# First tokens' gated product made early in C12's bank, and the completing product moved to second place

## The chip, the cores and the metric

The kernel runs on one core of one Trainium2 chip. The metric is the device time of one execution in microseconds; three runs of the kernel before took 3023.33, 3024.01 and 3027.07 us, median 3024.01. TensorE multiplies (PE in the profile; PEld is its weight loader), VectorE (DVE), ScalarE (ACT) and GpSimd (POOL) work on elements, SyncE (SP) issues DMAs. Each engine takes its instructions in order and waits at the first one that is not ready.

## The reference

Eight sequences of 3072 tokens by 256 features pass a Fourier mixing layer and then a gated feed-forward layer:

```python
X = np.fft.rfft(x, axis=1)
Yr = Xr @ w_r - Xi @ w_i + b_r ;  Yi = Xr @ w_i + Xi @ w_r + b_i
Yr, Yi = softshrink(Yr, 0.01), softshrink(Yi, 0.01)
y = np.fft.irfft(Yr + 1j * Yi, n=3072, axis=1)          # (8, 3072, 256)
out = ((y @ w_a) * (y @ w_b)) @ w_out                   # d_ff = 1536
```

## The kernel before

The Fourier part of a batch runs in small tasks: `f1` (16 of three 512-column matmuls), `f2` (12), `f3` (12 times two halves), `i1` (12) and `i2` (16). The feed-forward part takes most of TensorE's time. It works on pairs of token blocks of 2 x 384 tokens (32 pairs, four a batch) and, for each pair, on 12 blocks of 128 of the 1536 features: 384 steps, the function `step`. A step makes both gates a and b of its block for both halves of the tokens, a 2 x 2 block product, with seven products in place of eight (Strassen's scheme in Winograd's form).

A product, `run(k)`, is three matmuls of 384 columns (`mm3`: every operand is split in a high and a low half). The seven accumulate in three PSUM banks: X (two alternate, `x_ps`), `ya` and `yb`. Between them ScalarE copies a bank as it then stands to SBUF (`take`: s1, s2, s5) and VectorE adds. In the program before the order is

- run(0) into X, copy s1; run(1) into ya, c11 = s1 + ya (VectorE, in s1); a slot; `last_prod` of the step before;
- run(2) into X, copy s2; run(3) into yb, copy s5; output piece 0 of the step before; a slot;
- run(4) into X, then c22 = s5 + X (VectorE); run(5) into yb; output pieces 1 to 3 of the step before;
- then for the first 384 tokens: Y = yb + s2 in the bank, s1 = Y * s1 in SBUF (the gated product), and its split: ScalarE writes the high half h1, VectorE the low half l1 = s1 - h1.

`last_prod` adds the seventh product to X one step later, and makes the gated product and the split (h2, l2) of the last 384 tokens. Both halves of the tokens stand side by side in one tile g, a high one and a low one, of which there is one buffer (pool `p1`). `proj` multiplies g by a block of `w_out`, in four output pieces of three matmuls (the table `pieces`: bank, place in it, half of the 256 output features, first token, tokens); the third matmul of a piece is the one that reads the low half of g. The pieces collect over the 12 steps of a pair in three more banks.

A slot runs the next Fourier task. There are two in a step. Of the 372 steps after the first pair, 262 have a task in the second slot and 110 have none (75 of them have none in the first either); in 63 steps the first holds f2 and the second i1, and these follow steps that hold the two halves of f3.

The order on TensorE is that of the code. The order on the other engines is set by `Order`: a chain of operations is handed over where its input is issued; its urgent operations are issued when a model of the engines' times says that they can start, and the others when the model finds an engine free, or when `put` or `need` asks for them. `vacate` and `reads` say which operation of a chain is the last reader of a bank.

The result tile's pieces are copied out by `store` at the end of a pair. In the first pair (before 265 us) VectorE also decodes the feed-forward weights.

Of the kernel before, what the change touches and what calls it, by code (L numbers as in the profile page):

```python
# [12 lines left out]
F32 = mybir.dt.float32  # L13
# [9 lines left out]
P = 128  # L23
NJ = DFF // P
W = 384
# [230 lines left out]
def fft_mix_glu_kernel(ctx: ExitStack, tc: tile.TileContext, x, w_r, w_i, b_r, b_i, w_a, w_b, w_out, c1, m2, v, t2, out):  # L256
# [416 lines left out]
    def yr_sums(p):  # L673
        for k in ((0, 0), (0, 1), (1, 0)):
            od.put(yr[k][1])
        a11, a12, a21, a22 = (yr[k][0] for k in ((0, 0), (0, 1), (1, 0), (1, 1)))
        s3 = p6.tile([P, W], F32, tag="yr", name="yr")
        s2 = p6.tile([P, W], F32, tag="yr", name="yr")
        yr["c"] = od.chain(
            ("V", W, lambda e: tt(e, s3, a11, a21, ALU.subtract)),  # L680
            ("V", W, lambda e: tt(e, a21, a21, a22, ALU.add)),
            ("V", W, lambda e: tt(e, s2, a21, a11, ALU.subtract)),
            ("S", 0, lambda e: [yr_split(p, k) for k in range(RING - 7 if p else 0)]),
            spare=True,
        )
        yr["s"] = [a11, a12, s2, a21, s3, a12, a22]
        yr["pair"] = p
# [9 lines left out]
    def yr_split(p, k, urgent=0):  # L697
        if p == 0 and k < 2:
            s, c = yr[0, k]
            od.put(c)  # L700
        else:
            od.put(yr["c"], 1)
            s = yr["s"][k]
        h = state["ring"].tile([P, W], F32R, tag="ych", name="ych")
        l = state["ring"].tile([P, W], F32R, tag="ycl", name="ycl")
        ops = split(W, s, h, l)
        if k == 5:
            od.put(yc[p, 1][2])
            ops.insert(0, ("V", W, lambda e: tt(e, s, s, yr["s"][2], ALU.subtract)))
        yc[p, k] = h, l, od.chain(*ops, urgent=urgent, spare=True)  # L710
# [10 lines left out]

    weight_of = (0, 1, 5, 4, 6, 3, 2)
    gs = {}
# [11 lines left out]

    pieces = ((1, 2 * P, 1, 0, 2 * P), (0, 0, 0, 0, 4 * P), (2, 0, 1, 2 * P, 4 * P), (1, 0, 0, 4 * P, 2 * P))

    def proj(p, j, i):
# [11 lines left out]
        if j == 0:  # L750
# [6 lines left out]
            l[:, tok : tok + n],  # L757
            j == 0 and i < 3,
            j == NJ - 1,
# [6 lines left out]
    def store(p):  # L766
        osb = [p2.tile([P, 2 * W], F32, tag="osb", name="osb") for _ in range(2)]

        def take(d, tok, k, at, n):
            return ("AV", n, lambda e: copy(e, osb[d][:, tok : tok + n], o_ps[k][:, at : at + n]))  # L770

        def put(d):
            to = out[d * P : (d + 1) * P, 2 * W * p : 2 * W * (p + 1)]
            return ("S", 0, lambda e: nc.sync.dma_start(to, osb[d]))

        mid = 2 * P
        c = od.chain(
            take(0, 2 * mid, 1, 0, mid),
            take(1, 0, 1, mid, mid),
            take(0, 0, 0, 0, 2 * mid),  # L780
            put(0),
            take(1, mid, 2, 0, 2 * mid),
            put(1),
        )
        for k, left in enumerate((3, 4, 1)):
# [20 lines left out]
    def step(n, nxt):  # L806
# [26 lines left out]
        run(0, X, True)  # L833
        s1, c1_ = take(X)
        od.vacate(ya)
        run(1, ya, True)
        c11 = od.chain(add(s1, ya), urgent=1)
        od.reads(ya, c11, 0)
        slot()
        if n:  # L840
            last_prod(pp, pj)
        od.need(c1_)
# [6 lines left out]
        slot()  # L849
        od.need(c2_)  # L850
        run(4, X)
        od.put(c5_)
        held[p, j] = X, s5, od.chain(add(s5, X), urgent=1)
        od.need(c5_)
        run(5, yb)
        for i in range(1, 4):
            proj(pp, pj, i)
        if n:
            od.put(gs.pop((pp, pj))[3])
        h, l = (p1.tile([P, 2 * W], F32R, tag="g" + x, name="g") for x in "hl")  # L860
# [3 lines left out]
            ("V", W, lambda e: tt(e, Y, Y, s2, ALU.add)),  # L864
            ("V", W, lambda e: tt(e, s1, Y, s1, ALU.mult)),
            *split(W, s1, h1, l1, "VG"),
            urgent=2,
        )
        od.reads(yb, c, 2)
        gs[p, j] = [h, l, c, None]  # L870

    def f1_tasks(b):
# [190 lines left out]
```

## Time and profile before

| | |
|---|---|
| median of three runs | 3024.01 us |
| the profiled execution, its time | 3023.87 us |
| its span, first to last instruction | 3022.0 us |
| mean granted TensorE clock | 0.985 of full speed |
| busy: TensorE, VectorE, ScalarE, GpSimd | 2893.2, 2049.5, 1454.2, 874.1 us |

The rows below are from that one execution. A step takes some 6 to 8 us, by the tasks in its slots. Matmuls are pipelined: the listed duration of a matmul is longer than the distance to the next one, so lost time is read from distances between starts, or from the gaps of the weight loader (PEld).

### The profile page before, as it was taken

Reading aid. Unit: us, or ns where it says so; the run is one execution under the profiler, and the core shown is the slowest. Engines: PE = TensorE matmul, PEld = TensorE weight load, DVE = VectorE, ACT = ScalarE, POOL = GpSimd, SP = SyncE. Lnnn points to the kernel's source line nnn. Section 1 sums busy time; section 2 is a strip of 40 time slices with the busy share of each in tenths; the row PEclk is TensorE's granted clock in tenths of the full one; section 3 lists DMA queues with packets and bytes.
Section 4 is the critical chain, followed back from the end, with each engine's and each line's share of the span. In section 5 each row is a group of like instructions: output and inputs, shape, how many; then the busy total and the mean of one; then the engine's idle time right before and its main releaser. Section 6 shows DMA issues by size and latency. Waiting matters only on the chain.

```text
span 3022.0 us, 45662 instructions
## 1 busy us (share of the span) xinstructions
PE 2893.2 (96%) x16936; PEld 2667.2 (88%) x16936; DVE 2049.5 (68%) x3740; ACT 1454.2 (48%) x3226; POOL 874.1 (29%) x789
## 2 busy tenths in 40 slices
PE   5689999999999999999999999999999999999999
PEld 3568999899989999899998999989999899999998
DVE  7897676576765677666676676756676576766665
ACT  5454444544445444454445444454444544444443
POOL 4453331333322333223332223232232332310000
PEclk7889999999999999999999999999999999999999
DMA  6342111311113111221113211132112311110000
GB/s 184 117 123 69 55 36 54 94 59 57 41 51 109 39 61 36 78 83 39 55 39 100 73 41 46 56 95 62 52 36 62 94 57 52 41 40 26 26 11 22
DMA packets 123616, 186.55 MB, mean 62 GB/s; under 512 B 12320, under 2 KB 80768, under 8 KB 123392
## 3 DMA queue, kind: packets, MB, share of 16 engines
q1 hardware_dynamic: 120976, 177.26, 19.2%
q10 hardware_dynamic: 2416, 6.37, 0.7%
q8 instruction: 133, 2.18, 0.3%
q14 instruction: 91, 0.75, 0.1%
HBM read 108.08 MB, written 75.50 MB: 61 GB/s over the span
## 4 chain that ended last, share of the span: by engine, by line
PE 60%; issue 15%; DVE 12%; POOL 7%; ACT 5%; DMA 2%; DVEq 0%; ACTq 0%; POOLq 0%; SPq 0%
PE bank L290 60%; DVE g L284 3%; POOL zy L284 3%; POOL sx L284 2%; DVE s L284 2%; DVE zy L284 1%; ACT g L370 1%; DVE yr L284 1%; DVE bank L284 1%; POOL xs L284 1%; ACT s L824 1%; ACT sx L540 1%; POOL ycl L284 1%; ACT sx L534 0%; DMA m_in<-const_m_dram 0%
## 5 line engine op out<-in xcount | busy, mean ns | idle before, releaser
L824 ACT COPY s<-bank 128x384 f32<-128x384 f32 x1152 | 552.0, 484 | 1161.1 <-PE bank L290 1157.0
L284 DVE TENSOR_TENSOR s<-bank,s 128x384 f32<-128x384 f32 x1152 | 629.2, 556 | 535.3 <-PE bank L290 441.9
L284 DVE TENSOR_TENSOR bank<-bank,s 128x384 f32<-128x384 f32 x768 | 430.7, 561 | 49.9 <-PE bank L290 34.4
L284 POOL TENSOR_TENSOR ycl<-yr,ych 128x384 fp32r<-128x384 f32 x184 | 204.9, 1128 | 708.7 <-ACT ych L370 557.9
L284 DVE TENSOR_TENSOR g<-bank,g 128x384 fp32r<-128x384 f32 x384 | 213.1, 555 | 214.4 <-ACT g L799 214.4
L284 DVE TENSOR_TENSOR g<-s,g 128x384 fp32r<-128x384 f32 x384 | 268.7, 700 | 73.3 <-ACT g L370 71.2
L284 POOL TENSOR_TENSOR zy<-zy,zc 128x512 f32<-128x512 f32 x84 | 108.1, 1287 | 644.5 <-DVE zc L615 644.5
L284 POOL TENSOR_TENSOR x<-xin,x 96x512 fp32r<-96x512 f32 x104 | 137.6, 1323 | 414.7 <-PE bank L290 229.9
L290 PE MATMUL bank<-ych,wc2l 128*128 128x384 f32 x672 | 237.1, 353 | 2.2 <-DVE s L284 2.2
L290 PE MATMUL bank<-ych,wc0l 128*128 128x384 f32 x672 | 232.8, 346 | 3.2 <-ACT s L824 2.0
L290 PE MATMUL bank<-ych,wc3l 128*128 128x384 f32 x672 | 232.7, 346 | 0.8 <-DVE s L284 0.6
L290 PE MATMUL bank<-ych,wc1l 128*128 128x384 f32 x672 | 229.8, 342 | 0.0
L290 PE MATMUL bank<-ycl,wc0h 128*128 128x384 f32 x672 | 227.0, 338 | 0.0
L290 PE MATMUL bank<-ych,wc0h 128*128 128x384 f32 x672 | 226.8, 337 | 0.0
L290 PE MATMUL bank<-ycl,wc2h 128*128 128x384 f32 x672 | 226.5, 337 | 0.0
L290 PE MATMUL bank<-ycl,wc3h 128*128 128x384 f32 x672 | 226.3, 337 | 0.0
L290 PE MATMUL bank<-ycl,wc1h 128*128 128x384 f32 x672 | 226.3, 337 | 0.0
L290 PE MATMUL bank<-ych,wc2h 128*128 128x384 f32 x672 | 226.1, 337 | 0.0
L290 PE MATMUL bank<-ych,wc3h 128*128 128x384 f32 x672 | 226.0, 336 | 0.0
L290 PE MATMUL bank<-ych,wc1h 128*128 128x384 f32 x672 | 226.0, 336 | 0.0
L290 PE MATMUL bank<-wm_h,sx 128*128 128x256 f32 x1152 | 221.9, 288 | 4.0 <-DVE sx L284 4.0
L370 ACT CAST g<-s 128x384 fp32r<-128x384 f32 x384 | 197.6, 514 | 42.5 <-DVE s L284 39.9
(187 smaller groups left out, 6893.8 us busy)
## 6 DMA issues: line engine op xcount, KB each, us to landing
xin<-in_x_dram SPq DMA_DIRECT2D x128, 192.0 KB, 2.8
g_d<-gst SPq DMA_DIRECT2D x128, 192.0 KB, 2.1
gt<-g_d SPq DMA_DIRECT2D x96, 256.0 KB, 2.8
d_d<-dst SPq DMA_DIRECT2D x96, 256.0 KB, 2.1
dt<-d_d SPq DMA_DIRECT2D x64, 384.0 KB, 4.1
out_dram<-osb SPq DMA_DIRECT2D x64, 384.0 KB, 2.4
m_in<-const_m_dram SPq DMA_DIRECT2D x96, 128.0 KB, 2.1
t_in<-const_t_dram SPq DMA_DIRECT2D x64, 144.0 KB, 2.4
```

The lines of the kernel that those rows point to most:

```text
L284: (nc.vector if e == "V" else nc.gpsimd).tensor_tensor(o, a, b, op=op)
L290: nc.tensor.matmul(o, lhsT=l, rhs=r, start=start, stop=stop, **kw)
L370: ("a", n, lambda e: nc.scalar.copy(hi, w)),
L540: ("A", 512, lambda e: nc.scalar.copy(xh2, xsf)),
L824: return s, od.chain(("A", W, lambda e: nc.scalar.copy(s, q[:, :W])), urgent=1)
```

## The change

Seven things move. (1) run(4) and run(5) change places in the meaning of their operands: the one that completes C12 in yb now comes first, with its own weights and input (the list `yr["s"]` and `weight_of`; the difference a12 - s2 is now made for input 4). (2) The gated product of the first 384 tokens starts right behind it: Y + s2 and the product with s1 both stay in the bank yb, ScalarE casts h1 from the bank, and VectorE subtracts l1 from the bank. GpSimd is no choice for l1 any more. (3) The bank yb is now free for the next run(3) when l1 is done; before, when the product was in SBUF. (4) Output pieces are regrouped: pieces 0 and 1 take tokens 0 to 255 (256 columns each, one bank), pieces 2 and 3 tokens 256 to 767 (512 columns each). (5) Piece 1 moves ahead of run(4), pieces 2 and 3 stay last. (6) `last_prod` comes second in a step, right after run(0). (7) `store` copies by the new pieces.

```diff
--- before.py
+++ after.py
@@ -683,7 +683,7 @@
             ("S", 0, lambda e: [yr_split(p, k) for k in range(RING - 7 if p else 0)]),
             spare=True,
         )
-        yr["s"] = [a11, a12, s2, a21, s3, a12, a22]
+        yr["s"] = [a11, a12, s2, a21, a12, s3, a22]
         yr["pair"] = p
 
     def yr_have(p):
@@ -704,7 +704,7 @@
         h = state["ring"].tile([P, W], F32R, tag="ych", name="ych")
         l = state["ring"].tile([P, W], F32R, tag="ycl", name="ycl")
         ops = split(W, s, h, l)
-        if k == 5:
+        if k == 4:
             od.put(yc[p, 1][2])
             ops.insert(0, ("V", W, lambda e: tt(e, s, s, yr["s"][2], ALU.subtract)))
         yc[p, k] = h, l, od.chain(*ops, urgent=urgent, spare=True)
@@ -719,7 +719,7 @@
             t()
         return t is not None
 
-    weight_of = (0, 1, 5, 4, 6, 3, 2)
+    weight_of = (0, 1, 5, 4, 3, 6, 2)
     gs = {}
 
     def prod(p, j, k, ps, start):
@@ -733,7 +733,7 @@
         mm3(ps[:, :W], h[:, i, f : f + P], l[:, i, f : f + P], yh, yl, start, True, skip_group_check=True)
 
 
-    pieces = ((1, 2 * P, 1, 0, 2 * P), (0, 0, 0, 0, 4 * P), (2, 0, 1, 2 * P, 4 * P), (1, 0, 0, 4 * P, 2 * P))
+    pieces = ((1, 0, 0, 0, 2 * P), (1, 2 * P, 1, 0, 2 * P), (0, 0, 0, 2 * P, 4 * P), (2, 0, 1, 2 * P, 4 * P))
 
     def proj(p, j, i):
 
@@ -755,7 +755,7 @@
             ol[:, d * P : (d + 1) * P],
             h[:, tok : tok + n],
             l[:, tok : tok + n],
-            j == 0 and i < 3,
+            j == 0 and i != 1,
             j == NJ - 1,
             before=lambda: od.need(c),
             skip_group_check=True,
@@ -766,22 +766,15 @@
     def store(p):
         osb = [p2.tile([P, 2 * W], F32, tag="osb", name="osb") for _ in range(2)]
 
-        def take(d, tok, k, at, n):
+        def take(i):
+            k, at, d, tok, n = pieces[i]
             return ("AV", n, lambda e: copy(e, osb[d][:, tok : tok + n], o_ps[k][:, at : at + n]))
 
         def put(d):
             to = out[d * P : (d + 1) * P, 2 * W * p : 2 * W * (p + 1)]
             return ("S", 0, lambda e: nc.sync.dma_start(to, osb[d]))
 
-        mid = 2 * P
-        c = od.chain(
-            take(0, 2 * mid, 1, 0, mid),
-            take(1, 0, 1, mid, mid),
-            take(0, 0, 0, 0, 2 * mid),
-            put(0),
-            take(1, mid, 2, 0, 2 * mid),
-            put(1),
-        )
+        c = od.chain(take(0), take(1), take(2), put(0), take(3), put(1))
         for k, left in enumerate((3, 4, 1)):
             od.reads(o_ps[k], c, left)
 
@@ -832,13 +825,13 @@
         od.vacate(X)
         run(0, X, True)
         s1, c1_ = take(X)
+        if n:
+            last_prod(pp, pj)
         od.vacate(ya)
         run(1, ya, True)
         c11 = od.chain(add(s1, ya), urgent=1)
         od.reads(ya, c11, 0)
         slot()
-        if n:
-            last_prod(pp, pj)
         od.need(c1_)
         run(2, X)
         s2, c2_ = take(X)
@@ -847,27 +840,30 @@
         s5, c5_ = take(yb)
         proj(pp, pj, 0)
         slot()
-        od.need(c2_)
-        run(4, X)
-        od.put(c5_)
-        held[p, j] = X, s5, od.chain(add(s5, X), urgent=1)
+        proj(pp, pj, 1)
         od.need(c5_)
-        run(5, yb)
-        for i in range(1, 4):
-            proj(pp, pj, i)
+        run(4, yb)
         if n:
-            od.put(gs.pop((pp, pj))[3])
+            od.put(gs[pp, pj][3])
         h, l = (p1.tile([P, 2 * W], F32R, tag="g" + x, name="g") for x in "hl")
         h1, l1, Y = h[:, :W], l[:, :W], yb[:, :W]
         od.put(c11)
         c = od.chain(
             ("V", W, lambda e: tt(e, Y, Y, s2, ALU.add)),
-            ("V", W, lambda e: tt(e, s1, Y, s1, ALU.mult)),
-            *split(W, s1, h1, l1, "VG"),
+            ("V", W, lambda e: tt(e, Y, Y, s1, ALU.mult)),
+            ("A", W, lambda e: nc.scalar.copy(h1, Y)),
+            ("V", W, lambda e: tt(e, l1, Y, h1.bitcast(F32), ALU.subtract)),
             urgent=2,
         )
-        od.reads(yb, c, 2)
+        od.reads(yb, c, 0)
         gs[p, j] = [h, l, c, None]
+        od.need(c2_)
+        run(5, X)
+        od.put(c5_)
+        held[p, j] = X, s5, od.chain(add(s5, X), urgent=1)
+        for i in range(2, 4):
+            proj(pp, pj, i)
+        gs.pop((pp, pj), None)
 
     def f1_tasks(b):
         return [lambda u=u: f1(b, u) for u in range(16)]
```

What this makes of the order on three engines, in one place of the program. First TensorE, step 75 (f2 in its first slot, i1 in its second): before, from output piece 0 (bank_79) and i1 (zh, zl) to the two products.

```order
L290 MATMUL bank_79<-g,wo2l 128x256
L290 MATMUL bank_79<-g,wo2h 128x256 x2
L290 MATMUL bank_85<-zh,v_sb 128x512 x2
L290 MATMUL bank_85<-zl,v_sb 128x512
L290 MATMUL bank_82<-ych,wc1l 128x384
L290 MATMUL bank_82<-ych,wc1h 128x384
L290 MATMUL bank_82<-ycl,wc1h 128x384
L290 MATMUL bank_84<-ych,wc1l 128x384
L290 MATMUL bank_84<-ych,wc1h 128x384
L290 MATMUL bank_84<-ycl,wc1h 128x384
```

After it, the same place:

```order
L290 MATMUL bank_79<-g,wo2l 128x256
L290 MATMUL bank_79<-g,wo2h 128x256 x2
L290 MATMUL bank_85<-zh,v_sb 128x512 x2
L290 MATMUL bank_85<-zl,v_sb 128x512
L290 MATMUL bank_79<-g,wo2l 128x256
L290 MATMUL bank_79<-g,wo2h 128x256 x2
L290 MATMUL bank_84<-ych,wc1l 128x384
L290 MATMUL bank_84<-ych,wc1h 128x384
L290 MATMUL bank_84<-ycl,wc1h 128x384
L290 MATMUL bank_82<-ych,wc1l 128x384
L290 MATMUL bank_82<-ych,wc1h 128x384
L290 MATMUL bank_82<-ycl,wc1h 128x384
```

Piece 1 stands in front of the two products, and the product into bank_84 (yb) in front of that into bank_82 (X).

VectorE, from the zy operations of f3 in step 74 to step 75: before. Here bank6 is yb, s_7045 holds s1 and then the gated product, g_7119 the low halves, s_7080 is s5.

```order
L284 TENSOR_TENSOR zy_7093<-bank7_85,bias_88 64x256 x2
L284 TENSOR_TENSOR s_7080<-bank3_81,s_7080 128x384
L284 TENSOR_TENSOR zy_7093<-bank7_85,k_7066 64x256 x2
L615 TENSOR_SCALAR zc_7094<-zy_7093 128x512
L284 TENSOR_TENSOR bank6_84<-bank6_84,s_7075 128x384
L284 TENSOR_TENSOR s_7045<-bank6_84,s_7045 128x384
L284 TENSOR_TENSOR s_7125<-bank5_83,s_7125 128x384
L284 TENSOR_TENSOR g_7119<-s_7045,g_7118 128x384
L284 TENSOR_TENSOR bank3_81<-bank3_81,s_7080 128x384
L284 TENSOR_TENSOR g_7119<-bank3_81,g_7118 128x384
```

And with the change (s_7046 is s1, s_7082 is s5, g_7106 the low halves):

```order
L284 TENSOR_TENSOR zy_7093<-bank7_85,bias_88 64x256 x2
L284 TENSOR_TENSOR zy_7093<-bank7_85,k_7072 64x256
L284 TENSOR_TENSOR bank6_84<-bank6_84,s_7077 128x384
L284 TENSOR_TENSOR zy_7093<-bank7_85,k_7072 64x256
L284 TENSOR_TENSOR s_7082<-bank3_81,s_7082 128x384
L284 TENSOR_TENSOR bank6_84<-bank6_84,s_7046 128x384
L615 TENSOR_SCALAR zc_7094<-zy_7093 128x512
L284 TENSOR_TENSOR g_7106<-bank6_84,g_7105 128x384
L284 TENSOR_TENSOR bank3_81<-bank3_81,s_7082 128x384
L284 TENSOR_TENSOR s_7124<-bank5_83,s_7124 128x384
L284 TENSOR_TENSOR g_7106<-bank3_81,g_7105 128x384
```

The two operations on bank6 now stand between and right behind the zy operations, c22 (s_7082) between them, and l1 (g_7106 from bank6) ahead of last_prod's product (bank3) and of c11 (s_7124).

ScalarE, step 75 before: s_7125 is s1, g_7118 takes h1 and h2, s_7155 is s2, s_7161 is s5.

```order
L824 COPY s_7125<-bank4_82 128x384
L370 CAST zh_7095<-zy_7093 128x512
L370 CAST g_7118<-s_7045 128x384
L281 COPY xs_7143<-bank7_85 128x512
L540 CAST sx_7141<-xs_7143 128x2x256
L824 COPY s_7155<-bank4_82 128x384
L824 COPY s_7161<-bank6_84 128x384
L799 CAST g_7118<-bank3_81 128x384
```

And with the change: g_7105 takes h1 from bank6 and h2 from bank3, s_7154 is s2, s_7160 is s5.

```order
L854 CAST g_7105<-bank6_84 128x384
L817 COPY s_7124<-bank4_82 128x384
L792 CAST g_7105<-bank3_81 128x384
L281 COPY xs_7148<-bank7_85 128x512
L817 COPY s_7154<-bank4_82 128x384
L370 CAST zh_7095<-zy_7093 128x512
L817 COPY s_7160<-bank6_84 128x384
```

h1 stands in front of s1, h2 in front of s2, and zh has moved between s2 and s5.

## Rows read from the trace of the kernel before

**Rows 1.** The page: engine, busy us, share, instructions.
```profile
PE 2893.2 (96%) x16936; PEld 2667.2 (88%) x16936; DVE 2049.5 (68%) x3740; ACT 1454.2 (48%) x3226; POOL 874.1 (29%) x789
```

**Rows 2.** Busy by stage: us, PE, PEld, DVE, ACT, POOL, clock, DMA.
```profile
155.00:265.00 110.00, 93.76 (x458) 79.78 (x458) 98.44 (x173) 61.26 (x139) 54.70 (x54) 0.92 0.37 108
265.00:3022.00 2757.00, 2702.15 (x16037) 2511.20 (x16035) 1833.26 (x3354) 1318.65 (x2934) 752.49 (x673) 1.00 0.18 55
```

**Rows 3.** Loader's waits, 265 us on: total us, times, longest.
```profile
PEld bank L290 <- DVE g L284: 81.4, 164, 2.7
PEld bank L290 <- ACT g L370: 11.8, 15, 0.8
PEld bank L290 <- ACT s L824: 8.6, 36, 0.7
PEld bank L290 <- DVE s L284: 1.9, 7, 0.6
```

**Rows 4.** Waits of the weight loader, 155 to 265 us.
```profile
PEld bank L290 <- DVE g L284: 13.5, 12, 3.4
```

**Rows 5.** Timeline, step 75: start, duration, engine, operation, [idle before].
```profile
747.07 1.29 POOL L284 TENSOR_TENSOR zl<-zy,zh 128x512 fp32r<-128x512 f32 x1 [0.73 <-ACT zh L370]
...
747.44 1.34 DVE L284 TENSOR_TENSOR g<-s,g 128x384 fp32r<-128x384 f32 x1 [0.82 <-ACT g L370]
...
748.36 0.28 PE L290 MATMUL bank<-g,wo2h 128*128 128x256 f32 x1
...
748.62 1.31 POOL L284 TENSOR_TENSOR sx<-xs,sx 128x512 fp32r<-128x512 f32 x1 [0.26 <-ACT sx L540]
...
748.83 0.19 PEld L290 LDWEIGHTS bank<-g,wo2h 128*128 128x128 f32 x1 [0.40 <-DVE g L284]
748.84 0.38 PE L290 MATMUL bank<-g,wo2h 128*128 128x256 f32 x1 [0.20 <-DVE g L284]
...
749.80 0.56 DVE L284 TENSOR_TENSOR g<-bank,g 128x384 fp32r<-128x384 f32 x1 [0.54 <-ACT g L799]
```

**Rows 6.** Groups by shape, 265 us on: count, busy us, mean ns, idle before.
```profile
L824 ACT COPY s<-bank 128x384 f32<-128x384 f32 x1116 | 534.9, 484 | 1142.7 <-PE bank L290 1142.3
L284 DVE TENSOR_TENSOR bank<-bank,s 128x384 f32<-128x384 f32 x746 | 418.4, 561 | 49.6 <-PE bank L290 34.1
L284 DVE TENSOR_TENSOR g<-s,g 128x384 fp32r<-128x384 f32 x373 | 258.7, 694 | 73.3 <-ACT g L370 71.2 <-PE bank L290 1.1
...
L284 DVE TENSOR_TENSOR g<-bank,g 128x384 fp32r<-128x384 f32 x373 | 207.0, 555 | 214.4 <-ACT g L799 214.4
...
L799 ACT CAST g<-bank 128x384 fp32r<-128x384 f32 x373 | 181.1, 485 | 1.1 <-DVE bank L284 1.1
...
L284 DVE TENSOR_TENSOR zy<-bank,k 64x256 f32<-64x256 f32 x168 | 71.1, 423 | 2.3
...
L540 ACT CAST sx<-xs 128x512 fp32r<-128x512 f32 x84 | 52.3, 623 | 2.2
```

**Rows 7.** Timeline, step 94.
```profile
894.83 1.34 DVE L284 TENSOR_TENSOR yr<-yr 128x384 f32<-128x384 f32 x1
...
897.15 0.19 PEld L290 LDWEIGHTS bank<-g,wo9h 128*128 128x128 f32 x1 [2.73 <-DVE g L284]
```

**Rows 8.** Timeline, steps 106 and 107, whose slots are empty.
```profile
981.86 0.44 PE L290 MATMUL bank<-ych,wc3l 128*128 128x384 f32 x1
...
982.14 0.34 PE L290 MATMUL bank<-ych,wc3h 128*128 128x384 f32 x1
...
984.01 0.40 PE L290 MATMUL bank<-g,wo9h 128*128 128x256 f32 x2
...
984.24 0.33 PE L290 MATMUL bank<-ych,wc3l 128*128 128x384 f32 x1
...
984.58 0.34 PE L290 MATMUL bank<-ycl,wc3h 128*128 128x384 f32 x1
...
984.96 0.48 ACT L824 COPY s<-bank 128x384 f32<-128x384 f32 x1 [3.15 <-PE bank L290]
```

## The prediction

> **What bounds the kernel now.** I read the page first, then the busy time by stage, the waits of TensorE's weight loader, single steps of the timeline, and the groups of operations for durations.
>
> The page says that TensorE is busy for 96% of the span [rows 1]: only its gaps and its own work can be saved, and the change leaves its matmuls as many and as long as they were (four output pieces of 256, 256, 512 and 512 columns in place of 256, 512, 512 and 256). The table by stage shows where gaps are left [rows 2]. Up to 265 us the start and the first pair run (granted clock 0.92 from 155 us on); from 265 us to the end, 372 steps, the clock is 1.00, so nothing is to be had from it there.
>
> A stalled matmul shows best at the weight loader, since the matmul before it still drains and hides part of the gap. From 265 us the loader waits 81.4 us for VectorE and 11.8 us for ScalarE to finish g, 8.6 for a copy s, 1.9 for VectorE's s: 103.7 us together [rows 3]. Rows 5 show that a loader gap is about the time lost: the third matmul of output piece 0 starts 0.48 us after the second where 256 columns take 0.12, and its loader gap is 0.40.
>
> Why it waits there is in the same rows. The low half of g (l1) is a subtraction of two SBUF tiles. It began at 747.44 while GpSimd's zl ran (747.07 for 1.29 us) and took 1.34 us. The low half for the last tokens, at 749.80, has a PSUM bank as one source; it ran beside GpSimd's sx (748.62 for 1.31 us) and took 0.56 us [rows 5]. Over all steps the two groups average 694 and 555 ns [rows 6]. So g is late for two reasons: its chain starts only after run(5) and the pieces, and its last operation is slowed by GpSimd.
>
> **The change part by part.** I count a step from the first matmul of run(4) in the new order. From rows: 0.17 us a 384-column matmul and 0.115 a 256-column one (984.01, 984.24, 984.58 [rows 8]), so 0.52 a product; a 512-column one as twice 256 (0.23), 0.70 a piece. A bank is read 0.38 us after the start of its product's third matmul (984.58 to 984.96), and a tile read 0.05 after the write that it waits for (748.78 to 748.83 [rows 5]).
>
> *The early chain.* Y+s2 starts at 0.34+0.38 = 0.72. Two VectorE operations in the bank (0.56 each [rows 6]) end the product at about 1.9. The high half (0.485) must also wait for the second matmul of piece 3, which still reads the only g buffer: 0.52+0.52+0.70+0.23+0.4 = 2.4. So h1 ends at 2.9 and l1 (0.555) at 3.5. run(3) of the next step, which overwrites the bank, arrives after run(5), two pieces, run(0), last_prod, run(1), run(2): 0.52+0.52+1.4+4x0.52 = 4.5, or later with work in the first slot. The margin is 1.0 us, so the g waits of piece 0 go.
>
> In the steps that lost most (f3 in the second slot, f2 in the next step) VectorE has four zy operations (0.42 each) and the two bank operations and c22 in one row. With the order shown above, c22 ends at about 2.7 and last_prod needs it at 0.52+0.52+1.4+0.52 = 2.96; l1 ends at about 4.5, against run(3) at 4.5 plus f2. No wait here.
>
> *last_prod second, late pieces last.* The chain of the last tokens starts one product and a slot earlier, and the first piece that needs it (piece 2) comes after both run(4) and run(5). From the third matmul of last_prod: 0.38+0.56+0.05+0.485+0.1+0.555 = 2.1 until l2, against 0.17+3x0.52+0.70+2x0.52+0.47 = 3.9 for the matmul that reads it. The 2.73 us wait once a batch, where three yr sums of up to 1.34 us stood ahead of l2 [rows 7], goes too; the sums now stand ahead of Y+s2.
>
> *What is late next.* run(4) now reuses the bank yb, so it waits for the copy s5 of run(3). Between them stand piece 0, the second slot and piece 1. With an empty slot: 0.17+6x0.115 = 0.86 from the third matmul of run(3), against 0.38+0.484+0.05 = 0.91 for the copy: 0.05 late, and a load that could not be made ahead costs 0.11 more (981.86 to 982.14 is 0.28 in place of 0.17 [rows 8]). By the work lists 110 of the 372 steps have an empty second slot: 110 x 0.16 = 17 us. Bounds: 0 if the load is not late, 0.35 a step (39 us) if ScalarE comes one operation late. I take 17, from the nearest rows.
>
> Smaller items. In some 30 of these steps two ych casts stand ahead of s2 and s5 on ScalarE: 0.2 more, 6 us. Where f2 and i1 fill the slots (63 steps) ScalarE has xs, s2, zh, s5 in a row from the end of f2: 0.35+0.62+0.46+0.6+0.48 = 2.5 against 0.6+0.52+0.35+0.7+0.35 = 2.5 for run(4), so 0 to 0.3; I take 0.05, 3 us, as VectorE and ScalarE start an operation a little before the last one's listed end. In 6 steps the first f2 puts a cast of 0.62 ahead of s5 and some 1.7 us of small VectorE operations ahead of l1: about 1.2 each, 7 us. In 6 steps the yr sums make c22, the next h2 and s5 late: about 1.7 each, 10 us. Four pair ends of the last batch have output copies in the way: 2 us. New waits: 17+6+3+7+10+2 = 45 us.
>
> [...] The subtraction l1 now has a PSUM source where both were SBUF tiles. By the two groups [rows 6] that takes the mean from 694 to 555 ns, 52 us less work on VectorE, and off the path while the margin of 1.0 us holds. [...]
>
> *First pair.* VectorE is busy for 98 of its 110 us [rows 2] and the loader waits 13.5 us for its g [rows 4]. Less work on l1 helps, more is in front of it: I take 6 off; bounds 8 lost and 14 won.
>
> **The sum.** 103.7 gone, 45 new, 6 from the first pair: 65 us less. The profiled execution took 3023.87 us (span 3022.0), the median of the runs shown is 3024.01. 3023.9 - 65 = 2959 us.
>
> **The rivals.**
> *s5 decides.* ScalarE's queue is the new bottleneck: h2 and a long FFT cast stand ahead of s5, run(4) waits 0.35 in the 110 and in the 63 steps. That adds 22 and 19 us: 3000. For it: the margin of 0.0 in the f2 steps. Against it: ScalarE is busy for 1319 of 2757 us [rows 2], and the order shown has h2 in front of s2 by a product or more.
> *yb is freed too late, slower.* l1 is now the last reader of yb. If it stood behind last_prod's product and c11 on VectorE, which wait for TensorE, it would end 0.38+0.56+0.56+0.55 = 2.05 after the third matmul of run(1), where run(3) comes 0.7 after it when the first slot is empty (82 steps) and 1.4 after it with a task of 0.7 us there (62): 82x1.35 + 62x0.65 = 151 us lost, so 2959+151 = 3110. With c11 alone ahead it is 0.56 less each: 82x0.8 + 62x0.1 = 72, 3031. It decides once l1 is over 1.0 us later than worked out. The order has l1 in front in nearly all steps, so this needs a chain much slower than the rows.
> *Only moved.* VectorE itself, not the place of the chain, makes g late, and what leaves piece 0 returns at run(3) and run(4): 3015 to 3024. Against it: VectorE is busy for 1833 of 2757 us [rows 2].
>
> **How the numbers follow.** Forecast 80%, s5 12%, yb 5%, only moved 3%. A measurement here tells about 0.2% (6 us) from no change, so faster 0.92, same 0.03, slower 0.05. The forecast's own bounds: 17 less if the s5 load is in time and 8 more off the first pair, 2934; with 22 for the empty slots and 10 for the rest, 2991. I give 2936 to 2992.
>
> **What would show it.** In the profile after: loader waits for g below 15 us from 265 us on; waits of 0.05 to 0.2 us for the ScalarE copy s, some hundred, in the steps without a second task; the group g<-bank of 746 on VectorE near 555 ns and no group g<-s; VectorE's busy time about 50 us less. It is wrong if waits for a copy s take more than 50 us, or if run(3) waits for g.

## The result: 2.5% faster, and the profile after

The changed kernel takes 2949.46 us (median of 4 runs, 2946.18 to 2950.15) against 3024.61 us (4 runs, 3023.33 to 3027.07): a ratio of 0.9748, 95% interval 0.9732 to 0.9765. That is 75 us less, where 65 were forecast. The profiled execution has a span of 2947.9 us.

The page after, in the columns of [rows 1]:

```profile
PE 2859.5 (97%) x16936; PEld 2675.0 (91%) x16936; DVE 1897.2 (64%) x3710; ACT 1481.5 (50%) x3226; POOL 894.2 (30%) x819
```

TensorE's matmuls are as many as before. Its busy time fell by 34 us, since part of a stall is listed as busy (the matmul at 981.86 [rows 8] has 0.44 us for the usual 0.34, and in front of 748.84 [rows 5] the loader's gap is 0.40 and TensorE's 0.20); VectorE's fell by 152.

The busy time by stage, in the columns of [rows 2]. The first pair now ends at 260 us, so the stages are cut there:

```profile
155.00:260.00 105.00, 88.46 (x452) 77.52 (x452) 94.81 (x174) 60.34 (x141) 57.55 (x56) 0.93 0.39 112
260.00:2948.00 2688.00, 2672.03 (x16039) 2520.96 (x16037) 1683.70 (x3323) 1346.14 (x2932) 769.94 (x701) 1.00 0.18 56
```

The granted clock of the second stage is 1.00 as before. The first pair's stage lost little of its length; the 372 steps behind it hold nearly all of the gain.

The waits of TensorE's weight loader in those steps, against [rows 3]:

```profile
PEld bank L290 <- ACT s L817: 12.3, 32, 0.5
PEld bank L290 <- POOL sx L284: 8.0, 14, 0.6
PEld bank L290 <- DVE sx L557: 2.0, 7, 0.3
PEld bank L290 <- DVE s L284: 0.7, 2, 0.3
PEld bank L290 <- DVE g L284: 0.5, 2, 0.3
PEld bank L290 <- ACT g L792: 0.5, 1, 0.5
```

The 81.4 and 11.8 us for g are 0.5 and 0.5. What is left waits for the copies s of ScalarE and for the Fourier operand sx, which GpSimd makes.

The groups by shape, against [rows 6]:

```profile
L284 DVE TENSOR_TENSOR bank<-bank,s 128x384 f32<-128x384 f32 x1117 | 629.3, 563 | 644.1 <-PE bank L290 551.1 <-ACT dst L281 81.9
L817 ACT COPY s<-bank 128x384 f32<-128x384 f32 x1116 | 531.8, 484 | 208.0 <-PE bank L290 200.1 <-ACT g L792 0.3
L284 DVE TENSOR_TENSOR g<-bank,g 128x384 fp32r<-128x384 f32 x746 | 414.1, 557 | 168.9 <-ACT g L854 140.7 <-PE bank L290 12.6 <-ACT g L792 6.7
...
L284 DVE TENSOR_TENSOR yr<-yr 128x384 f32<-128x384 f32 x120 | 76.9, 641 | 1.0
```

Every subtraction into g now has a bank as its source, 746 of them at 557 ns, and no group g<-s is left. The sums yr, which the change doesn't touch, take 641 ns in place of these:

```profile
L284 DVE TENSOR_TENSOR yr<-yr 128x384 f32<-128x384 f32 x121 | 121.4, 1003 | 4.3 <-DVE yr L284 0.5
```

A loader's wait is not the whole of a stall, so I also took the start of each matmul less that of the one before, and less the usual spacing of its kind (0.174 us for 384 columns, 0.118 for 256, 0.233 for 512), summed over each step. Of these sums, items (a product, an output piece, a task) with no more than 0.06 us, which I don't count as waits, make 4 us before and 10 after. Mean us lost in a step, by the tasks in its two slots, and the sum over the 372 steps:

| slots: first, second (steps) | before | after |
|---|---|---|
| f2, i1 (63) | 0.62 | 0.04 |
| none, none (75) | 0.43 | 0.18 |
| f2 or i2, none (21) | 1.31 | 0.50 |
| i1, none (14) | 0.42 | 0.23 |
| first half of f3, second half (77) | 0.02 | 0.09 |
| the same for the batch's first (u = 0), 18 matmuls in place of 12 (7) | 0.03 | 0.89 |
| all 372 | 114.1 us | 46.6 us |
| the 12 steps of the first pair | 30.2 us | 26.9 us |

From the start of step 12 (264.57 us before, 259.95 after) to that of step 383 (3006.02 and 2933.84) the time fell from 2741.4 to 2673.9 us: 67.6 of the 74.1 us of span. Steps 0 to 12 gave 3.3, the start 1.3 and the end 1.9.

### The profile page after: what moved, and what is told of

Read it like the earlier page. It is cut to its first block, busy times and chain, and to the rows that moved or that the text cites. A ratio compares the mean times of both kernels' runs of the same rounds, so it can differ in the third digit from the quotient of the medians.

```text
span 2947.9 us, 46775 instructions
## 1 busy us (share of the span) xinstructions
PE 2859.5 (97%) x16936; PEld 2675.0 (91%) x16936; DVE 1897.2 (64%) x3710; ACT 1481.5 (50%) x3226; POOL 894.2 (30%) x819
## 3 DMA queue, kind: packets, MB, share of 16 engines
q1 hardware_dynamic: 120976, 177.26, 19.7%
## 4 chain that ended last, share of the span: by engine, by line
PE 85%; ACT 3%; POOL 1%; DVE 1%; issue 1%; DMA 0%; SPq 0%; DVEq 0%; ACTq 0%; POOLq 0%
PE bank L290 85%; ACT s L817 1%; DVE bank L284 1%; POOL sx L284 1%; DVE zy L284 0%; ACT xs L281 0%; POOL ycl L284 0%; POOL zl L284 0%; POOL xs L284 0%; ACT zh L370 0%; ACT osb L281 0%; DVE s L284 0%; ACT g L792 0%; ACT ych L370 0%; ACT g L854 0%
## 5 line engine op out<-in xcount | busy, mean ns | idle before, releaser
L284 DVE TENSOR_TENSOR bank<-bank,s 128x384 f32<-128x384 f32 x1152 | 648.9, 563 | 649.5 <-PE bank L290 556.2
L854 ACT CAST g<-bank 128x384 fp32r<-128x384 f32 x384 | 184.9, 481 | 830.2 <-DVE s L284 513.7
L284 DVE TENSOR_TENSOR g<-bank,g 128x384 fp32r<-128x384 f32 x768 | 426.3, 557 | 170.4 <-ACT g L854 142.0
L284 DVE TENSOR_TENSOR s<-bank,s 128x384 f32<-128x384 f32 x768 | 424.3, 552 | 12.0 <-PE bank L290 1.2
L792 ACT CAST g<-bank 128x384 fp32r<-128x384 f32 x384 | 184.9, 482 | 220.8 <-DVE bank L284 220.8
L284 POOL TENSOR_TENSOR x<-xin,x 96x512 fp32r<-96x512 f32 x110 | 147.1, 1339 | 387.6 <-ACT x L370 200.3
```

The costliest lines, as they stand in the source:

```text
L284: (nc.vector if e == "V" else nc.gpsimd).tensor_tensor(o, a, b, op=op)
L792: ("A", W, lambda e: nc.scalar.copy(h, X)),
L854: ("A", W, lambda e: nc.scalar.copy(h1, Y)),
```

## The experiments

The theory to be tested was that of the forecast: l1 comes late for piece 0 for two reasons, a chain that starts late and a subtraction slowed beside GpSimd, and each part of the change takes its own share; what is left is run(4)'s wait for the copy s5. The main rivals were that one part alone carries the gain, and that VectorE's work as such sets the time. Each experiment has its time beside the kernel before on the same chip (medians 3024.25 to 3024.81 us); all ratios are to that.

### Each part alone, or undone

**The completing product second, nothing else.** In the kernel before:

```diff
         s1, c1_ = take(X)
+        if n:
+            last_prod(pp, pj)
         od.vacate(ya)
...
         slot()
-        if n:
-            last_prod(pp, pj)
         od.need(c1_)
```

> The kernel before with one edit: the completing product of C22 stands second in a step, after run(0), in place of fourth. Theory (each part of the change takes its own share of the g waits): the low half for the last tokens is ready one product and one slot earlier, so the waits of piece 1 (0.8 us in the 21 steps with a long first task and an empty second slot, 17 us) and most of the six waits of 2.7 us behind the yr sums (16 us) go, and the waits of piece 0, which reads the first tokens alone, stay: 2990 to 3005 us, loader waits for VectorE's g from 81 down to 45 to 60 us. Rival (the place of this product is only carried along by the change): 3018 to 3025 us, loader waits for g unchanged.

Measured: 2996.42 us, ratio 0.9906 (0.9893 to 0.992). The loader's wait for l1 and l2:

```profile
PEld bank L290 <- DVE g L284: 56.3, 122, 0.8
```

It fell from 81.4 to 56.3 us. The wait of piece 1 in the 21 steps with f2 or i2 and an empty second slot went from 0.82 us to 0.00, and most of that of piece 0 stayed (0.23 in the empty steps for 0.17, 0.38 with f2 and i1 for 0.52). So this move alone takes 28 us off, inside the theory's range, but in part by luck. Six of the 21 steps are those behind the yr sums, and their 15 us stand twice in the theory's working. The 372 steps lost 20 us less, and the first pair with the start, which the theory left out, gave 7.

**The product and its split in the bank, nothing else.** In the kernel before:

```diff
-            ("V", W, lambda e: tt(e, s1, Y, s1, ALU.mult)),
-            *split(W, s1, h1, l1, "VG"),
+            ("V", W, lambda e: tt(e, Y, Y, s1, ALU.mult)),
+            ("A", W, lambda e: nc.scalar.copy(h1, Y)),
+            ("V", W, lambda e: tt(e, l1, Y, h1.bitcast(F32), ALU.subtract)),
...
-        od.reads(yb, c, 2)
+        od.reads(yb, c, 0)
```

> The kernel before with one edit: the first tokens' gated product is written into run(5)'s bank and its low half is subtracted from there on VectorE; the order of products and pieces is as before. Theory (lateness has two causes, a late start and a subtraction slowed beside GpSimd): the waits of piece 0 where zl runs beside it (63 steps of 0.6 us, 39 us) go, since a 0.56 us subtraction replaces one of 1.34, and about a third of the others: 2970 to 2990 us. Rival one (the order alone decides): 3015 to 3025 us. Rival two (the bank alone decides, the moved products are paid back by the new waits for s5): 2945 to 2955 us, as the changed kernel.

Measured: 3079.24 us, ratio 1.0182 (1.0168 to 1.0195): 55 us slower, outside all three. The loader's waits, and an empty step at 993 us:

```profile
PEld bank L290 <- DVE g L284: 151.7, 162, 2.7
```

```profile
992.50 0.55 DVE L284 TENSOR_TENSOR g<-bank,g 128x384 fp32r<-128x384 f32 x1
...
993.10 0.19 PEld L290 LDWEIGHTS bank<-ych,wc3l 128*128 128x128 f32 x1 [0.92 <-DVE g L284]
```

The wait for g has nearly doubled, and it stands at another place: the load is one for a product (ych), run(3), which overwrites the bank that l1 still reads. By steps, piece 0 waits 0.00 in the empty steps and run(3) 0.96; in the f2 and i1 steps 0.00 and 0.72. So the late chain, and not only the slow subtraction, made g late, and with l1 reading the bank the lateness is met 0.76 us sooner, at run(3) and not at the third matmul of piece 0 (three starts of 0.174 and two of 0.118).

**The order as changed, the product in SBUF.** In the changed kernel:

```diff
-            ("V", W, lambda e: tt(e, Y, Y, s1, ALU.mult)),
-            ("A", W, lambda e: nc.scalar.copy(h1, Y)),
-            ("V", W, lambda e: tt(e, l1, Y, h1.bitcast(F32), ALU.subtract)),
+            ("V", W, lambda e: tt(e, s1, Y, s1, ALU.mult)),
+            *split(W, s1, h1, l1, "VG"),
...
-        od.reads(yb, c, 0)
+        od.reads(yb, c, 2)
```

> The changed kernel with one part undone: the gated product goes to an SBUF tile and its low half is subtracted there by VectorE or GpSimd, as in the kernel before; order of products and pieces as changed. Theory: the chain starts about two pieces and a product earlier, so a 1.34 us subtraction is still in time for piece 0 in most steps (it ends 4.3 to 5.3 us after the first matmul of run(4), piece 0 comes at 5.4): 2950 to 2965 us, with 5 to 20 us of loader waits for g. Rival (the subtraction in the bank is what helps): 2995 to 3015 us, with over 50 us of loader waits for g.

Measured: 3017.04 us, ratio 0.9977 (0.9967 to 0.9986). The theory's time was wrong by over 50 us. The rival's time was nearly right (it ended at 3015), but its reason was wrong: nothing waits for g any more. The largest waits of the loader, and step 75:

```profile
PEld bank L290 <- ACT s L817: 35.8, 88, 1.5
PEld bank L290 <- ACT xs L281: 32.3, 56, 0.6
```

```profile
742.03 1.28 POOL L284 TENSOR_TENSOR zy<-zy,zc 128x512 f32<-128x512 f32 x1 [6.76 <-DVE zc L615]
...
742.28 1.45 DVE L284 TENSOR_TENSOR g<-s,g 128x384 fp32r<-128x384 f32 x1 [0.32 <-ACT g L370]
...
743.65 0.55 DVE L284 TENSOR_TENSOR bank<-bank,s 128x384 f32<-128x384 f32 x1
...
744.24 0.48 ACT L792 CAST g<-bank 128x384 fp32r<-128x384 f32 x1 [1.61 <-DVE bank L284]
...
744.62 0.59 ACT L281 COPY xs<-bank 128x512 f32<-128x512 f32 x1
...
745.26 0.30 PEld L290 LDWEIGHTS bank<-zh,v_sb 128*128 128x128 f32 x2 [0.58 <-ACT xs L281]
```

GpSimd, a choice for l1 here and in the kernel before, took none of the 384 in either. l1 (742.28) now starts beside GpSimd's zy and takes 1.45 us in place of 0.56. It is still in time for piece 0. But the product of the last tokens stands behind l1 on VectorE and starts at 743.65, as l1 ends (in the changed kernel 0.47 us behind l1's start, here 1.37), ScalarE's h2 waits for it until 744.24, idle for 1.61 us, and behind h2 stand the copy xs (of f2's result, whose last matmul is listed to end at 743.48, out of the bank that i1 uses next; it starts at 744.62) and the copy s5. The task i1 waits 0.64 us for the one and run(4) 0.24 for the other, in 63 steps of this kind 0.49 and 0.18 on average. These 63 steps lost 0.70 us each in place of 0.04, 42 of the 68 us between the two kernels. There the slow subtraction costs through the queue behind it, not through the piece that reads it.

**The completing product fourth again.** The edit of the first experiment undone, in the changed kernel:

```diff
         s1, c1_ = take(X)
-        if n:
-            last_prod(pp, pj)
         od.vacate(ya)
...
         slot()
+        if n:
+            last_prod(pp, pj)
         od.need(c1_)
```

> The changed kernel with one part undone: the completing product of C22 stands fourth again, after run(1) and the first slot. Theory: in the changed order the first piece that needs the last tokens (piece 2) stands behind run(4) and run(5), 3.4 us after this product where its chain takes 2.1, so its place now matters little, and c22, which it waits for, has a product more time: 2944 to 2955 us. Rival (the place of this product carries a good part of the gain): 2965 to 2985 us, with waits of piece 2 for g.

Measured: 2963.61 us, ratio 0.9797 (0.9783 to 0.981): between the two ranges. Its waits, and an empty step:

```profile
PEld bank L290 <- ACT s L817: 32.6, 105, 0.5
PEld bank L290 <- DVE g L284: 16.6, 29, 1.9
```

```profile
952.56 0.48 ACT L792 CAST g<-bank 128x384 fp32r<-128x384 f32 x1
...
952.94 0.49 ACT L817 COPY s<-bank 128x384 f32<-128x384 f32 x1
...
953.48 0.19 PEld L290 LDWEIGHTS bank<-ych,wc3l 128*128 128x128 f32 x1 [0.30 <-ACT s L817]
```

Two prices: piece 2 waits for g in the six steps behind the yr sums (1.61 us each), and h2 (952.56) now stands between s2 and s5 on ScalarE, so run(4) loses 0.36 us in the empty steps in place of 0.17. Against that the first pair's 12 steps lost 19.7 us in place of 26.9, which the last set uses.

### The new wait of run(4), and the margin of l1

**Piece 1 behind run(5).** In the changed kernel:

```diff
         proj(pp, pj, 0)
         slot()
-        proj(pp, pj, 1)
         od.need(c5_)
         run(4, yb)
...
-        for i in range(2, 4):
+        for i in range(1, 4):
```

> The changed kernel with one part undone: output piece 1 stands behind run(5) again, so that only piece 0 and the second slot lie between run(3) and run(4), which overwrites run(3)'s bank. Theory (in the 110 steps with an empty second slot run(4) waits for ScalarE's copy s5): two fewer matmul starts' worth of cover, 0.35 us, lengthen the wait of each of these steps by 0.35: 38 us more, 2982 to 2992 us, with loader waits for the copy s of 35 to 55 us. Rival (the wait for s5 is hidden or ends by something else): 2946 to 2955 us.

Measured: 3018.61 us, ratio 0.9983 (0.9974 to 0.9992). Larger than expected: 69 us more than the changed kernel.

```profile
PEld bank L290 <- ACT s L817: 92.2, 208, 2.9
PEld bank L290 <- ACT xs L281: 20.8, 70, 0.7
```

```profile
978.60 0.45 PE L290 MATMUL bank<-ych,wc3l 128*128 128x384 f32 x1 [0.22 <-ACT s L817]
...
978.88 0.33 PE L290 MATMUL bank<-ych,wc3h 128*128 128x384 f32 x1
```

In the empty steps run(4) loses 0.51 us in place of 0.17 (the matmul at 978.60 starts 0.38 late, and the second 0.28 behind it): 0.34 more, as worked out. Over the 110 steps that is 42 us, where 38 were expected. Another 24 are not the cover: in the 63 steps with f2 and i1 the planner (the model in `Order`) now gives ScalarE the cast zh ahead of the copy xs, and i1 waits 0.37 for xs. The first pair lost 7.5 more, the 48 steps with two three-matmul tasks 7; some 10 came back elsewhere.

**Piece 2 ahead of run(4) as well, where the second slot is empty.**

```diff
-        slot()
-        proj(pp, pj, 1)
+        busy = slot()
+        for i in (1,) if busy else (1, 2):
+            proj(pp, pj, i)
...
-        for i in range(2, 4):
+        for i in (2, 3) if busy else (3,):
```

> The changed kernel with one addition: where the second slot is empty, piece 2 too stands ahead of run(4), 0.7 us more cover. Theory: the remaining waits of run(4) in these 110 steps (0.17, 0.48 and 0.23 us by class, 26 us together) go, and piece 2 still finds the last tokens' low half ready, worked out 0.8 us ahead: 2922 to 2932 us. Rival (the chain for the last tokens is not in time for the earlier piece 2, and the wait moves there): 2940 to 2955 us, with waits of piece 2 for g.

Measured: 2972.35 us, ratio 0.9828 (0.9814 to 0.9841): 23 us slower than the changed kernel. Its waits, and the second of two empty steps:

```profile
PEld bank L290 <- DVE s L284: 31.1, 91, 1.0
PEld bank L290 <- DVE g L284: 21.4, 26, 1.1
```

```profile
965.67 0.57 DVE L284 TENSOR_TENSOR bank<-bank,s 128x384 f32<-128x384 f32 x1 [0.40 <-PE bank L290]
...
966.26 0.56 DVE L284 TENSOR_TENSOR s<-bank,s 128x384 f32<-128x384 f32 x1
...
966.74 0.55 DVE L284 TENSOR_TENSOR g<-bank,g 128x384 fp32r<-128x384 f32 x1
...
967.34 0.19 PEld L290 LDWEIGHTS bank<-ych,wc3l 128*128 128x128 f32 x1 [0.98 <-DVE g L284]
```

The waits of run(4) went (0.01 us in the empty steps), as expected, but neither theory nor rival named what came: with one piece less behind run(5), c22 is late for the completing product (0.19 us a step) and l1 for run(3) (0.16). Here the planner put the product of the last tokens (965.67) and c11 (966.26) ahead of l1 (966.74), and run(3) waited 0.98. That is the forecast's slower rival, l1 behind last_prod's product and c11, brought about by 0.7 us.

**The low half made twice.** In the changed kernel:

```diff
             ("V", W, lambda e: tt(e, l1, Y, h1.bitcast(F32), ALU.subtract)),
+            ("V", W, lambda e: tt(e, l1, Y, h1.bitcast(F32), ALU.subtract)),
```

> The changed kernel with the subtraction that makes the first tokens' low half (in the bank) done twice, the same result both times: 0.56 us more on VectorE in each of the 384 steps, 208 us of work. Theory (1.0 us of margin before run(3), which overwrites the bank, and before piece 0): most steps lose nothing; the delay passes to the product of the last tokens and to ScalarE's copy behind it, which have less room, so some steps with inverse-transform tasks lose 0.1 to 0.3: 2949 to 2970 us. Rival one (no margin; run(3) waits for g): over 3010 us. Rival two (VectorE's work as such is on the path): near 3150 us.

Measured: 3009.57 us, ratio 0.995 (0.9937 to 0.9962): 60 us more than the changed kernel, with 171 us more of VectorE's busy time (2068.1 for 1897.2).

```profile
PEld bank L290 <- DVE g L284: 55.4, 85, 1.0
```

```profile
741.08 0.56 DVE L284 TENSOR_TENSOR bank<-bank,s 128x384 f32<-128x384 f32 x1
741.54 0.55 DVE L284 TENSOR_TENSOR s<-bank,s 128x384 f32<-128x384 f32 x1
...
742.01 1.01 DVE L284 TENSOR_TENSOR g<-bank,g 128x384 fp32r<-128x384 f32 x2
...
742.61 0.19 PEld L290 LDWEIGHTS bank<-ych,wc1l 128*128 128x128 f32 x1 [0.58 <-DVE g L284]
```

VectorE's work as such is not on the path one for one, but the margin is less than its length says: the second subtraction was not placed behind the first but behind the product and c11 (742.01 starts with it), so l1 came 1.4 us later and run(3) waited 0.62 us on average in the 63 steps like this one. In the empty steps it waited 0.00, and run(4) and the completing product lost 0.23 more. The test therefore moved l1 by more than it meant to.

**The completing product fourth in the first pair alone,** added to the kernel with piece 2 ahead:

```diff
-        if n:
+        if n and p:
             last_prod(pp, pj)
...
         slot()
+        if n and not p:
+            last_prod(pp, pj)
```

> The kernel of f2_more_cover with one more addition: in the first pair alone, whose steps from the twelfth back took 7 us less in the kernel with the completing product in fourth place, that product stands fourth. Theory: the steady state's gain of more cover, 17 to 27 us, and 5 to 8 us from the first pair: 2916 to 2926 us. Rival (the first pair's end only shifts work into the steps behind it): as f2_more_cover, within 3 us.

Measured: 2967.67 us, ratio 0.9811 (0.9798 to 0.9824). The steady state's gain wasn't there, as just told; the first pair gave 4.7 us.

### A version that beats both

The cover must come from ahead of run(3), so that nothing behind run(4) moves. Where the second slot will be empty, run(3) is issued ahead of run(2):

```diff
-        run(2, X)
-        s2, c2_ = take(X)
+        first = len(tasks)
+        if first:
+            run(2, X)
+            s2, c2_ = take(X)
         od.vacate(yb)
         run(3, yb, True)
         s5, c5_ = take(yb)
+        if not first:
+            run(2, X)
+            s2, c2_ = take(X)
```

> The changed kernel with one addition: where no task is left for the second slot, run(3) stands ahead of run(2), so run(2) too lies between run(3) and run(4), 0.52 us more cover for the copy s5, and nothing behind run(4) moves. Theory (in the kernel with piece 2 ahead the waits of run(4) went, and came back because run(4), the product of C22 and the first tokens' chain had less room behind them): here the waits of run(4), 26 us by class, go down to some 5, and run(3), 0.52 us earlier, meets a bank that is free in the 75 steps where both slots are empty (with the low half made twice it waited there 0.00) and waits 0.1 to 0.3 in the 35 others: 2928 to 2940 us. Rival (the low half is late for run(3) as in the kernel with piece 2 ahead): 2950 to 2975 us, with waits of run(3) for g.

Measured: 2944.52 us, ratio 0.9733 (0.972 to 0.9746). In the empty steps run(4) lost 0.06 us in place of 0.17. run(3) waited for g in six of them alone, 0.45 us each. But in 28 of the 35 steps with a first task (14 with f2, 14 with i1) run(4) still lost 0.57 and 0.24: there the work list holds an empty entry for the second slot, its length isn't zero, and run(2) stayed first. Only the seven with i2 had the exchange.

> The kernel of f6_swap_2_3 with the completing product in fourth place in the first pair alone. Theory: as in the kernels with piece 2 ahead, where this took 4.7 us off, 3 to 7 us less than f6_swap_2_3. Rival: within 2 us of it.

Measured, with the edit for the first pair: 2936.54 us, ratio 0.9709 (0.9696 to 0.9723), 8 us less than without it and a little over what was expected (the two profiled spans differ by 4.8); the first pair's steps lost 19.5 us in place of 26.0.

The condition mended, on top of the last:

```diff
-        first = len(tasks)
+        first = bool(tasks and tasks[0])
```

> The kernel of f7_swap_pair0 with the exchange of run(2) and run(3) also in the steps whose second slot holds an empty entry of the work list; there the two kernels with the exchange left run(2) first, and run(4) still waited 0.38 and 0.25 us in the 35 steps with a first task. Theory (cover of 0.52 us is worth up to the wait it covers): these waits go, up to 11 us, less what run(3), 0.52 us earlier, waits for the first tokens' low half in the same steps: 2924 to 2933 us. Rival (the low half is just in time there and the wait passes to run(3)): 2933 to 2940 us, with loader waits for VectorE's g of 10 us or more in place of 2.9.

Measured: 2924.18 us, ratio 0.967 (0.9657 to 0.9683). The loader's largest waits:

```profile
PEld bank L290 <- POOL sx L284: 7.9, 14, 0.6
PEld bank L290 <- DVE g L284: 3.9, 9, 0.5
```

No row for a copy s is left. (The 35 steps of the expectation are 28, since the seven with i2 had the exchange already.) The 372 steps lost 26.5 us in place of the changed kernel's 46.6, run(4) at most 0.01 in any kind of step. run(3) waits for g in the same six empty steps, 0.45 us each and 2.7 together, and in no other step with the exchange. It is 100 us faster than the kernel before, and 25 than the changed one.

Last, the completing product also fourth in the seven steps with u = 0 (`late` is set on that task):

```diff
-        if n and p:
+        late = not p or bool(tasks and getattr(tasks[0], "late", False))
+        if n and not late:
             last_prod(pp, pj)
...
-        if n and not p:
+        if n and late:
```

> The kernel of f8_swap_all with the completing product in fourth place also in the seven steps whose first slot holds the first spectral product of a batch (18 matmuls), which waits 0.85 us for its operands from GpSimd; with that product fourth in every step it waited 0.28. Theory: 7 x 0.57 = 4 us less than f8_swap_all. Rival: within 1.5 us of it, since the wait moves to run(4) or to the next step's product.

Measured: 2923.32 us, ratio 0.9665 (0.9652 to 0.9679), 0.9 us below the last and not told from it:

```profile
PEld bank L290 <- DVE xs L560: 4.7, 6, 0.8
PEld bank L290 <- POOL sx L284: 4.4, 7, 0.6
```

GpSimd's share of the wait fell from 7.9 to 4.4 us and 4.7 for VectorE's xs took its place: what it waits for is a chain of small operations over three engines, not the one that was late last.

## Why the forecast held, point by point

**The waits for g go.** 103.7 us of loader waits were to go from 265 us on. Those for g went to 1.0. In step 75 after, l1 runs beside GpSimd's zy, in 0.56 us:

```profile
728.12 1.28 POOL L284 TENSOR_TENSOR zy<-zy,zc 128x512 f32<-128x512 f32 x1 [6.76 <-DVE zc L615]
...
728.34 0.56 DVE L284 TENSOR_TENSOR g<-bank,g 128x384 fp32r<-128x384 f32 x1 [0.30 <-ACT g L854]
...
729.93 0.34 PE L290 MATMUL bank<-ych,wc1l 128*128 128x384 f32 x1
```

It ends at 728.90, 4.4 us after the first matmul of run(4) (724.50), where 4.5 was worked out for a step with the zy operations. run(3) comes at 729.93 without a wait, 1.03 behind. In the empty steps 106 and 107 l1 ends 3.6 us after run(4)'s first matmul and run(3) comes at 4.6 (3.5 and 4.5 worked out): the margin of 1.0.

**Two causes, each with its share** was the theory I took to the experiments, and it fell. By shares the bank should have gained on its own, and it lost 55 us; the order with the early completing product gained 7 of the 75. The parts need each other: the early chain makes the bank free in time, and the bank keeps l1 at 0.56 us where the early chain puts it beside zy. The forecast had both halves of this (the chain's place, and the price of a late l1 in its slower rival), but its sum didn't need them apart. Within the new order, the exchange of run(4) and run(5) and the regrouped pieces were not run apart from each other, so what each is worth stays open.

**run(4) waits for s5.** Forecast: 0.16 us in 110 steps, 17 us, and 6 for ych casts ahead. Measured: 25.8 us (75 steps of 0.17, 21 of 0.48, 14 of 0.23); some 10 of them, in the 21 steps, belong to the next items. An empty step:

```profile
956.48 0.90 ACT L817 COPY s<-bank 128x384 f32<-128x384 f32 x2
...
957.43 0.19 PEld L290 LDWEIGHTS bank<-ych,wc3l 128*128 128x128 f32 x1
957.43 0.45 PE L290 MATMUL bank<-ych,wc3l 128*128 128x384 f32 x1
...
957.72 0.34 PE L290 MATMUL bank<-ych,wc3h 128*128 128x384 f32 x1
```

The copies end at 957.38 (two in one row), the load starts at 957.43, the first matmul with it and the second 0.29 later where 0.17 is usual. 0.14 us are lost and the loader shows no wait for them: run(4) loses time in 110 steps, and its list above has 32 waits for s. So the "some hundred waits" that the forecast asked of that view could not show there, though they were in the time.

**First f2 of a batch:** 7 us forecast. Found twice as much in another form. In 14 steps a cast (sx or zh) stands ahead of s5 on ScalarE, 0.57 us each, 8 us (part of the 25.8). And the seven steps behind wait 0.84 us, 6 us, which the forecast did not have, for GpSimd's part of sx:

```profile
270.38 0.73 POOL L284 TENSOR_TENSOR sx<-xs,sx 128x256 fp32r<-128x256 f32 x1 [1.77 <-ACT sx L534]
...
271.15 0.19 PEld L290 LDWEIGHTS bank<-wm_h,sx 128*128 128x128 f32 x1 [0.51 <-POOL sx L284]
```

Another 5 us, 0.7 in seven steps, are also a wait for GpSimd's sx, in the first step of a new pair, where a split of ycl stands ahead of it in GpSimd's queue: the planner gave GpSimd 30 operations more (819 for 789).

**The yr sums** were the mis-sized term: 10 us forecast, 1.7 in each of 6 steps. In those six steps 0.34 is left, 2 us, and not by the sums: at run(4), where ScalarE has a cast of x, 0.62 us, ahead of s2 and s5. The sums take 641 ns in place of 1003, for in the new order fewer of them run beside GpSimd (42 of 120, by overlap of the spans, in place of 74 of 121; beside it they took 0.81 and 1.29 us on average, alone 0.55 and 0.56). The f2 and i1 steps lost nothing where 3 us were forecast.

**The sum.** Of the 114 us before, 110 are waits (104 by the loader's rows); after there are 37 (25.8, 5.9, 4.9) where 45 were forecast. The steady state gained 67.6 us where 59 were forecast; the first pair with the start gave 4.6 (6 forecast), the end 1.9. That the sum of the new waits came so near is in part luck: run(4)'s plain waits for s5 are 16 us (23 forecast), the sums with the f2 and i1 steps 2 (13 forecast), the first f2's casts 8 (7 forecast), and the 11 at GpSimd's sx were not forecast. VectorE's 152 us less, where 50 were forecast, are l1's 54 (268.7 to 214.4 us), the sums' 44 and some 38 of operations that moved to GpSimd; the rest I did not trace.

**The rivals.** "s5 decides" had the right wait but not its size: 0.35 us came only with piece 1 taken away. "yb is freed too late" did not happen, but two of the experiments brought it about, with 0.7 us less behind run(5) and with the low half made twice. The forecast called for a chain over 1.0 us late, and 0.7 sufficed, since the planner then lets other work pass l1.

**What l1 costs from a bank.** The forecast took 555 ns for it, from the group for the last tokens [rows 6]. Where no GpSimd operation overlapped it, the subtraction took 550 ns on average from SBUF (271 in the kernel before, from 265 us on) and 557 from a bank (515 after, for both halves of the tokens): 7 ns more.

## What to carry to other kernels

A faster operation and an earlier one can each be worthless or worse alone (here the bank alone cost 55 us, and the order without it gained 7 of 75): ask of each what it newly holds (here a bank) and what it newly runs beside, and who is queued behind it. A wait that is left can be covered from ahead of the waiting pair, by a swap that nothing behind it sees (here 2.7 us of new waits against 26 gone); moving work from behind it takes the cover away from the next chain (here 23 us slower, with piece 2 ahead). Look for small stalls in the starts of the matmuls, not in the loader's idle time alone (here run(4) lost time in 110 steps, and the loader's list has 32 waits for s).

## What the runs showed of the chip

- A VectorE subtraction of two SBUF tiles (128x384) took 0.55 us where no GpSimd operation overlapped it (271 cases in the kernel before, from 265 us on) and 1.15 on average, up to 1.34, where over 0.3 us of it ran beside one (90 cases); in the kernel with the new order and an SBUF source 1.45 at 742.28. With a bank as one source it took 0.54 to 0.56 in both cases (215 and 158 before). In both rows shown, 747.44 [rows 5] and 742.28 above, the slowed subtraction ended 0.42 us behind GpSimd's operation.
- Where a product's first matmul started with its load (957.43 above), the second started 0.28 or 0.29 us behind it in every such row shown, 0.11 over the usual 0.17, beside the wait itself.
